# Sending the block sums of v to the query blocks: 128-byte DMA rows against a VectorE copy and 3 KB rows

## The chip, the cores and the metric

The kernel runs on one core of one Trainium2 chip. The metric is the device time of one execution in microseconds (us), as a median over runs. A profiled execution gives the rows below: PE is TensorE, PEld its weight loads, DVE VectorE, ACT ScalarE, POOL GpSimd, SP the engine that issues most of the copies inside the chip's memory and all stores. L306 means line 306 of the kernel before.

## The reference, cut to what matters

Sparse attention over 4 batches of 8 heads, 768 positions and 64 columns, then one expert of a mixture of experts per batch.

```python
block, window = (32, 16)
k_sum = k.reshape(B, H, nb, block, D).max(axis=3)    # nb = 24 blocks
v_sum = v.reshape(B, H, nb, block, D).mean(axis=3)
scores_l = where(|i - j| < window, scale * q @ k.T, -1e9)
scores_s = scale * q @ k_sum.T + log(block)
a = softmax(concat([scores_l, scores_s]))
x = a @ concat([v, v_sum])                           # every query sees all 24 block sums
e = argmax(x.mean(positions) @ w_gate)               # one expert per batch
out = gate * (relu(x @ w1[e]) @ w2[e])
```

## The kernel before, in words

Every head's 768 queries are cut into 12 blocks of 64 (`NJ`). For one block the keys and values that count are 120 rows: its own 64 positions, 16 before and 16 after (the halo), and the 24 block sums. They lie on 120 partitions of the tile `vblk[NR, H, NJ, DP]`, two of them, used by even and odd batches; `DP` is 66, that is 64 columns of v, then the weight by which a row counts in the denominator (1, or 32 for a block sum), and a filler. The weights are written once, in `edges`, lines 154 and 155. The block sums stand on partitions 96 to 119 and are the same for all 12 query blocks of a head, so they lie there 12 times.

A batch is worked through in pairs of heads, four of them (`NP`). The steps of a pair, each a function that is called in an order written out by hand (`attn`, `weave`, `run`; nothing is reordered by a planner):

- `T_k` turns k by TensorE, and VectorE builds the tile `kaug` from it: the copy of line 258, maxima by lines 265 to 273, halos and block maxima by the copies of lines 276, 279 and 282.
- `V_sum` issues the two halo copies on SP (lines 111 and 115), sums v by 12 small products per pair (line 294), casts the sums to bf16 (`vs_sb`, line 303), and sends them on: one DMA on SP for each head (line 306), from 24 partitions, with a broadcast over the 12 query blocks. One such DMA is 288 rows of 128 bytes.
- `T_q` turns q (copies of lines 250 and 252), `S_tile` makes the scores of six query blocks (line 347), ScalarE takes their exponential (`aT`, line 357), and VectorE multiplies by the band mask (line 360; in batch 0 the mask is added by TensorE instead).
- `O_tile` is the product of `aT` and all 120 rows of `vblk` (line 372): 24 matmuls for six query blocks of two heads in two calls. It is what waits for the halo and for the block sums. VectorE then divides (`rv` and `xs`, lines 380 and 383), and `X_tile` turns the result (line 399).

In batch 0 `V_sum` runs pair by pair, one pair ahead of `O_tile` (`pre` in `attn`), so there are four calls with two DMAs each. In batches 1 to 3 it runs once for all four pairs, between the first `T_k` and the first `T_q`, so there are three calls with eight DMAs each. Between the attention steps of batches 1, 2 and 3 the steps of the expert of the batch before are woven in: `H_chunk` (line 477) and `O_chunk` (line 498). The loads of q, k, v (lines 91 and 104) and of the expert's weights (lines 439 and 442) are issued by POOL, which writes their descriptors; those of the next batch and of the weights are issued in one go after `gate`, just when `V_sum` of the next batch runs.

Of the kernel before, what the change touches and what calls it, by code (L numbers as in the profile page):

```python
# [12 lines left out]
BF16 = mybir.dt.bfloat16  # L13
# [9 lines left out]
def kernel(  # L23
# [10 lines left out]
    nc = tc.nc  # L34

    B, H, S, D = q.shape
# [6 lines left out]
    BLK = 32  # L43
    NB = S // BLK
    NJ = S // QB
# [3 lines left out]
    R_SUM = QB + 2 * HALO  # L49
    NR = R_SUM + NB  # L50
# [8 lines left out]
    DP = D + 2  # L59
# [5 lines left out]
    const = ctx.enter_context(tc.tile_pool(name="const", bufs=1))  # L65
# [15 lines left out]
    kaugs = [  # L81
        const.tile([128, NP, NJ, 128], BF16, name=f"kaug{i}") for i in range(2)
    ]


    nat = {}
# [22 lines left out]
    def halo(b, h0, h1):  # L109
        vb = vblks[b % NV]  # L110
        nc.sync.dma_start(
            vb[R_PRE : R_PRE + HALO, h0:h1, 1:NJ, :],
            vb[QB - HALO : QB, h0:h1, 0 : NJ - 1, :],
        )
        nc.sync.dma_start(
            vb[R_POST : R_POST + HALO, h0:h1, 0 : NJ - 1, :],
            vb[0:HALO, h0:h1, 1:NJ, :],
        )
# [78 lines left out]
    )  # L197

    masks = []

    def make_mask():
        lo = const.tile([R_SUM, 1], FP32, name="lo")
        t_a = const.tile([R_SUM, 1], FP32, name="t_a")

        nc.vector.tensor_scalar(
            out=lo, in0=pf[0:R_SUM, :], scalar1=float(R_PRE), scalar2=float(R_PRE + HALO),
            op0=ALU.is_ge, op1=ALU.mult,
        )
        nc.vector.tensor_scalar(
            out=t_a, in0=pf[0:R_SUM, :], scalar1=float(R_POST), scalar2=-float(QB),  # L210
            op0=ALU.is_ge, op1=ALU.mult,
        )
        nc.vector.tensor_tensor(out=lo, in0=lo, in1=t_a, op=ALU.add)
        nc.vector.tensor_scalar(
            out=lo, in0=lo, scalar1=-float(HALO - 1), scalar2=None, op0=ALU.add
        )
        u_f = const.tile([R_SUM, QB], FP32, name="u_f")
        nc.vector.tensor_scalar(
            out=u_f, in0=it_u, scalar1=lo[:, 0:1], scalar2=None, op0=ALU.subtract
        )  # L220
        u_hi = const.tile([R_SUM, QB], FP32, name="u_hi")
        nc.vector.tensor_scalar(
            out=u_hi, in0=u_f, scalar1=float(2 * HALO - 2), scalar2=None, op0=ALU.is_le
        )
        mask = const.tile([NR, QB], BF16, name="mask")
        nc.vector.memset(mask[R_SUM:NR, :], 1.0)
        nc.vector.scalar_tensor_tensor(
            out=mask[0:R_SUM, :], in0=u_f, scalar=0.0, in1=u_hi,
            op0=ALU.is_ge, op1=ALU.mult,
        )  # L230
        masks.append(mask.unsqueeze(1).to_broadcast([NR, 2 * NW, QB]))
# [55 lines left out]
    def V_sum(b, prs):  # L287
        def f():
            vb = vblks[b % NV]
            halo(b, 2 * prs[0], 2 * prs[-1] + 2)  # L290
            vs_ps = one_pool.tile([128, 2, D], FP32, name="vsps", tag="one")
            for j in range(NJ):
                for pr in prs:
                    nc.tensor.matmul(
                        vs_ps[BLK * pr : BLK * (pr + 1), :, :],
                        lhsT=bind[:, j, :],
                        rhs=vb[0:QB, 2 * pr : 2 * pr + 2, j, 0:D],
                        start=(j == 0),
                        stop=(j == NJ - 1),
                    )  # L300
            vs_sb = small.tile([128, 2, D], BF16, name="vs_sb")
            rs = slice(BLK * prs[0], BLK * prs[-1] + BLK)
            nc.vector.tensor_copy(vs_sb[rs], vs_ps[rs])
            for pr in prs:
                for hh in range(2):
                    nc.sync.dma_start(  # L306
                        vb[R_SUM:NR, 2 * pr + hh, :, 0:D],
                        vs_sb[BLK * pr : BLK * pr + NB, hh, :]
                        .unsqueeze(1)
                        .to_broadcast([NB, NJ, D]),  # L310
                    )
        return f

    def T_q(b, pr):
# [313 lines left out]
```

## Time and profile before

| | |
|---|---|
| median of 2 runs | 221.12 us (221.11 to 221.12) |
| the profiled execution | 222.96 us, of which the span is 221.2 us |
| busy: PE, DVE, ACT, POOL | 164.1, 103.8, 85.5, 40.0 us |
| engine shares of the chain that ended last | PE 44%, DMA 20%, DVE 17%, ACT 11% |
| DMAs of line 306 | 32, each 36 KB as 288 rows |

"Idle before" is the time in which an engine stood still just ahead of an instruction, and the name behind the arrow is what ended it. The chain that ended last is followed back from the last instruction; a piece of it named "DMA" begins when that DMA was issued and ends when it let the next instruction go.

### The profile page before, as it was taken

What the parts mean: (1) busy time and instruction counts of PE and PEld (TensorE: products, weight loads), DVE (VectorE), ACT (ScalarE), POOL (GpSimd) and SP (SyncE); (2) the same over time, 40 slices, a digit from 0 to 9 for tenths busy, and PEclk for the clock granted to TensorE, in tenths of its full rate; (3) what the DMA queues carried; (4) which work ended last, traced back from release to release, by engine and by line L of the source; (5) the groups of instructions that cost most, each with busy time, mean ns of one, the idle gap of its engine ahead of it and who ended that gap; (6) DMA issues with size and microseconds to landing.
All of it is one profiled execution on the core that took longest, in us unless ns stands there. A gap on an engine that the chain in (4) does not pass through costs nothing.

```text
span 221.2 us, 5022 instructions
## 1 busy us (share of the span) xinstructions
PE 164.1 (74%) x2094; PEld 97.8 (44%) x2104; DVE 103.8 (47%) x292; ACT 85.5 (39%) x185; POOL 40.0 (18%) x58
## 2 busy tenths in 40 slices
PE   0563983673358889709989789539987899999993
PEld 0453763452334545305444445224444555456541
DVE  5752583267564856704394647521658440210021
ACT  2131560622044475600426474502534765147411
POOL 7981000029400003900000005000000006000000
PEclk9999999999999999975899999955999999999998
DMA  6999997209999950999997403992222009993033
GB/s 59 144 168 200 172 157 109 47 3 127 188 214 153 166 87 9 151 211 206 129 235 202 81 3 48 150 207 38 95 92 98 1 3 94 185 273 115 0 149 135
DMA packets 57574, 27.12 MB, mean 123 GB/s; under 512 B 37072, under 2 KB 54480, under 8 KB 57552
## 3 DMA queue, kind: packets, MB, share of 16 engines
q0 software_dynamic: 42720, 17.83, 83.9%
q1 hardware_dynamic: 14832, 8.98, 17.8%
q8 instruction: 16, 0.26, 0.5%
q14 instruction: 6, 0.05, 0.1%
HBM read 35.67 MB, written 6.29 MB: 190 GB/s over the span
## 4 chain that ended last, share of the span: by engine, by line
PE 44%; DMA 20%; DVE 17%; ACT 11%; issue 3%; POOL 2%; SPq 1%; ACTq 0%; POOLq 0%; DVEq 0%
DMA vblk<-vs_sb 20%; PE o_ps L498 18%; PE hps L477 12%; ACT aT L357 4%; DVE kaug L258 4%; PE ops L372 4%; ACT xT L400 3%; PE qps L241 3%; DVE aT L360 2%; PE xps L399 2%; PE sc L347 2%; DVE t L265 2%; ACT hT L484 1%; DVE kmx L273 1%; SPq L306 1%
## 5 line engine op out<-in xcount | busy, mean ns | idle before, releaser
L477 PE MATMUL hps<-xT,w_sb 128*128 128x384 bf16 x256 | 50.3, 334 | 0.0
L498 PE MATMUL o_ps<-w_sb,hT 128*128 128x512 bf16 x182 | 49.2, 408 | 0.6 <-issue 0.4
L484 ACT ACTIVATE hT<-hps 128x384 bf16<-128x384 f32 x64 | 31.4, 491 | 24.3 <-PE hps L477 24.3
L372 PE MATMUL ops<-vblk,aT 120*64 120x65 bf16 x384 | 14.5, 222 | 33.8 <-DMA vblk<-vs_sb 25.4
L439 POOL DMA_DIRECT2D w_sb<-in_moe_w_dram x14 | 10.5, 760 | 144.0 <-PE hps L477 84.4
L357 ACT ACTIVATE aT<-sc 128x768 bf16<-128x768 f32 x32 | 26.0, 812 | 15.2 <-PE sc L347 14.2
L372 PEld LDWEIGHTS <-aT 120*64 120x64 bf16 x384 | 10.9, 132 | 40.9 <-issue 18.2
L477 PEld LDWEIGHTS <-w_sb 128*128 128x128 bf16 x256 | 22.1, 99 | 13.8 <-issue 0.7
L498 PEld LDWEIGHTS <-hT 128*128 128x128 bf16 x192 | 17.9, 103 | 19.3 <-issue 3.3
L360 DVE TENSOR_TENSOR aT<-aT,mask 120x768 bf16<-120x768 bf16 x24 | 13.3, 556 | 24.4 <-ACT aT L357 24.4
L513 ACT ACTIVATE o_sb<-o_ps,gcol 128x512 f32<-128x512 f32 x12 | 8.2, 687 | 41.9 <-PE o_ps L498 37.8
L400 ACT ACTIVATE xT<-xps 128x384 bf16<-128x384 bf16 x32 | 15.6, 490 | 21.8 <-PE xps L399 21.5
L508 DVE TENSOR_SCALAR o_sb<-o_ps,gcol 128x512 f32<-128x512 f32 x12 | 9.0, 750 | 25.5 <-PE o_ps L498 22.4
L383 DVE TENSOR_TENSOR xs<-ops,rv 128x384 bf16<-128x384 f32 x32 | 17.8, 558 | 1.1
L380 DVE RECIPROCAL rv<-ops 128x6 f32<-128x6 f32 x32 | 6.1, 190 | 25.8 <-PE ops L372 25.6
L258 DVE COPY kaug<-kps 128x768 bf16<-128x768 bf16 x16 | 15.2, 952 | 5.8 <-PE kps L241 5.8
L347 PE MATMUL sc<-qT,kaug 64*128 64x64 bf16 x384 | 13.4, 210 | 5.3 <-DVE qT L252 2.6
L347 PEld LDWEIGHTS <-kaug 64*128 64x128 bf16 x384 | 10.8, 107 | 12.8 <-issue 10.1
L399 PE MATMUL xps<-identb,xs 128*128 128x128 bf16 x96 | 12.9, 256 | 3.2 <-ACT qT L250 1.4
L241 PE MATMUL kps<-identb,k_nat 96*64 96x96 bf16 x256 | 11.1, 245 | 5.0 <-POOL it_p L129 5.0
L252 DVE COPY qT<-qps 128x768 bf16<-128x768 bf16 x12 | 11.4, 952 | 4.7 <-PE qps L241 4.6
L399 PEld LDWEIGHTS <-xs 128*128 128x128 bf16 x96 | 8.4, 111 | 9.6 <-issue 3.1
(71 smaller groups left out, 145.4 us busy)
## 6 DMA issues: line engine op xcount, KB each, us to landing
out_dram<-o_sb SPq DMA_DIRECT2D x24, 256.0 KB
w_sb<-in_moe_w_dram POOLq DMA_DIRECT2D x11, 512.0 KB, 10.9
k_nat<-in_k_dram POOLq DMA_DIRECT2D x3, 768.0 KB, 15.7
vblk<-in_v_dram POOLq DMA_DIRECT2D x6, 384.0 KB, 19.2
q_nat<-in_q_dram POOLq DMA_DIRECT2D x3, 768.0 KB, 23.1
w_sb<-in_moe_w_dram POOLq DMA_DIRECT2D x9, 256.0 KB, 5.6
vblk<-vs_sb SPq DMA_DIRECT2D x32, 36.0 KB
vblk<-vblk SPq DMA_DIRECT2D x6, 181.5 KB
```

The costliest lines, as they stand in the source:

```text
L241: nc.tensor.transpose(ps[hh * D : (hh + 1) * D, r, :], src[:, 2 * pr + hh, r * D : (r + 1) * D], identb[0:PR, 0:PR],)
L258: nc.vector.tensor_copy(ka[:, :, 0:QB].rearrange("q j (p r) -> q j p r", r=RR), ps.rearrange("q r (j p) -> q j p r", j=NJ),)
L347: nc.tensor.matmul(sc[:, hh, w * QB : (w + 1) * QB], lhsT=ka[rs, pr, j, :], rhs=qT[rs, j * QB : (j + 1) * QB], start=not on_pe, stop=not o ...
L357: nc.scalar.activation(aT, sc[:, :, 0:HB], ACT.Exp, scale=SCALE)
L360: nc.vector.tensor_tensor(out=av, in0=av, in1=masks[0], op=ALU.mult)
L372: nc.tensor.matmul(ops[w * QB : (w + 1) * QB, t, hh, :], lhsT=aT[0:NR, hh, c0 : c0 + QB], rhs=vb[0:NR, 2 * pr + hh, u * NW + 2 * t + w, 0 ...
L383: nc.vector.tensor_tensor(out=xs, in0=ops[:, :, :, 0:D], in1=rv.unsqueeze(3).to_broadcast([128, NW // 2, 2, D]), op=ALU.mult,)
L399: nc.tensor.transpose(xps[:, t * 128 : (t + 1) * 128], xs[:, t], identb)
L400: nc.scalar.activation(xT[b][:, pr, u * HB : (u + 1) * HB], xps, ACT.Copy, accum_out=red[b][:, pr, u : u + 1],)
L477: nc.tensor.matmul(hps[:, 0:HB], lhsT=w1_sb[:, dt, ft * 128 : (ft + 1) * 128], rhs=xT[b][:, dt, u * HB : (u + 1) * HB], start=(dt == 0), s ...
L484: nc.scalar.activation(hTs[b][:, ft, u * HB : (u + 1) * HB], hps[:, 0:HB], ACT.Relu)
L498: nc.tensor.matmul(o_ps, lhsT=hTs[b][:, ft, st * 128 : (st + 1) * 128], rhs=w2_sb[:, ft, :], start=(ft == 0), stop=(ft == NFT - 1),)
```

## The change

In batch 0 VectorE writes a pair's sums straight into `vblk`, with one copy that reads `vs_sb` 12 times over. In the other batches one VectorE copy of 128 partitions fills a new tile `vrep`, in which the sums already stand 12 times beside their weight column, and one DMA per pair moves 24 rows of 3,168 bytes (2 heads x 12 blocks x 66 columns x 2 bytes). The weight columns of `vrep` are written once, ahead of the first pair.

```diff
+    vrep = const.tile([128, 2, NJ, DP], BF16, name="vrep")
...
+    nc.vector.memset(vrep[:, :, :, D:DP], float(BLK))
...
             nc.vector.tensor_copy(vs_sb[rs], vs_ps[rs])
+            if len(prs) == 1:
+                pr = prs[0]
+                nc.vector.tensor_copy(
+                    vb[R_SUM:NR, 2 * pr : 2 * pr + 2, :, 0:D],
+                    vs_sb[BLK * pr : BLK * pr + NB]
+                    .unsqueeze(2)
+                    .to_broadcast([NB, 2, NJ, D]),
+                )
+                return
+            nc.vector.tensor_copy(
+                vrep[:, :, :, 0:D], vs_sb.unsqueeze(2).to_broadcast([128, 2, NJ, D])
+            )
             for pr in prs:
-                for hh in range(2):
-                    nc.sync.dma_start(
-                        vb[R_SUM:NR, 2 * pr + hh, :, 0:D],
-                        vs_sb[BLK * pr : BLK * pr + NB, hh, :]
-                        .unsqueeze(1)
-                        .to_broadcast([NB, NJ, D]),
-                    )
+                nc.sync.dma_start(
+                    vb[R_SUM:NR, 2 * pr : 2 * pr + 2, :, :],
+                    vrep[BLK * pr : BLK * pr + NB],
+                )
```

## Rows read from the trace of the kernel before

**Rows 1.** The page: chain by line, and two of its costliest groups.

```profile
DMA vblk<-vs_sb 20%; PE o_ps L498 18%; PE hps L477 12%; ACT aT L357 4%; DVE kaug L258 4%; PE ops L372 4%; ACT xT L400 3%; PE qps L241 3%; DVE aT L360 2%; PE xps L399 2%; PE sc L347 2%; DVE t L265 2%; ACT hT L484 1%; DVE kmx L273 1%; SPq L306 1%
...
L439 POOL DMA_DIRECT2D w_sb<-in_moe_w_dram x14 | 10.5, 760 | 144.0 <-PE hps L477 84.4
...
L258 DVE COPY kaug<-kps 128x768 bf16<-128x768 bf16 x16 | 15.2, 952 | 5.8 <-PE kps L241 5.8
```

**Rows 2.** The waits: us in total, times, longest us.

```profile
PE ops L372 <- DMA vblk<-vs_sb: 25.4, 9, 4.7
```

**Rows 3.** The chain in order of time, batches 2 and 3: start, us, what.

```profile
89.37 10.30 DMA vblk<-vs_sb
...
137.81 9.51 DMA vblk<-vs_sb
```

**Rows 4.** The timeline, two copies of line 276 and 282 in batch 1.

```profile
65.25 0.20 DVE L276 COPY kaug<-kaug 128x176 bf16<-128x176 bf16 x1
...
65.48 0.22 DVE L282 COPY kaug<-kmx 128x288 bf16<-128x288 bf16 x1
```

**Rows 5.** The timeline, batch 1, first pair.

```profile
54.47 2.75 POOL L104 DMA_DIRECT2D vblk<-in_v_dram  x2
...
54.98 0.92 DVE L276 COPY kaug<-kaug 128x176 bf16<-128x176 bf16 x1
...
56.01 0.55 DVE L360 TENSOR_TENSOR aT<-aT,mask 120x768 bf16<-120x768 bf16 x1
...
58.94 0.20 DVE L380 RECIPROCAL rv<-ops 128x6 f32<-128x6 f32 x1 [2.39 <-PE ops L372]
```

**Rows 6.** The timeline, batch 0, first pair: start, us, engine, line, [idle before].

```profile
13.85 2.71 POOL L104 DMA_DIRECT2D vblk<-in_v_dram  x2
...
15.45 0.28 DVE L303 CAST vs_sb<-vsps 32x128 bf16<-32x128 f32 x1
...
19.54 1.23 PE L372 MATMUL ops<-vblk,aT 120*64 120x65 bf16 x24 [4.73 <-DMA vblk<-vs_sb]
...
20.48 0.20 DVE L380 RECIPROCAL rv<-ops 128x6 f32<-128x6 f32 x1 [4.74 <-PE ops L372]
```

**Rows 7.** The DMA queues from 11.8 to 15.0 us: packets, MB, share.

```profile
q1 hardware_dynamic: 132, 0.10, 11.8%
```

**Rows 8.** The timeline, batch 0, third pair.

```profile
33.97 0.30 DVE L303 CAST vs_sb<-vsps 32x128 bf16<-32x128 f32 x1
...
37.60 0.20 DVE L380 RECIPROCAL rv<-ops 128x6 f32<-128x6 f32 x1 [3.33 <-PE ops L372]
```

**Rows 9.** The timeline, first pairs of batch 2 and, last row, of batch 3.

```profile
88.50 12.87 SPq L306 DMA_DIRECT2D vblk<-vs_sb  x8
...
97.70 0.27 PE L372 MATMUL ops<-vblk,aT 120*64 120x65 bf16 x2 [4.70 <-DMA vblk<-vs_sb]
...
99.71 0.82 PE L372 MATMUL ops<-vblk,aT 120*64 120x65 bf16 x22 [1.74 <-DMA vblk<-vs_sb]
...
145.42 0.27 PE L372 MATMUL ops<-vblk,aT 120*64 120x65 bf16 x2 [4.02 <-DMA vblk<-vs_sb]
```

**Rows 10.** Stretches: us, busy (instructions) of PE, PEld, DVE, ACT, POOL, clock, DMA.

```profile
93.00:97.60 4.60, 0.00 (x1) 0.00 (x0) 1.40 (x6) 0.58 (x2) 1.53 (x2) 0.90 1.37 209
97.60:100.00 2.40, 0.56 (x13) 0.47 (x15) 0.00 (x0) 0.00 (x0) 0.00 (x0) 0.50 1.39 213
...
141.00:145.00 4.00, 0.40 (x3) 0.01 (x1) 1.59 (x7) 0.97 (x2) 0.00 (x0) 0.93 1.27 192
```

**Rows 11.** The timeline, the same five PE steps after batch 2's wait, and later.

```profile
100.97 0.61 PE L498 MATMUL o_ps<-w_sb,hT 128*128 128x512 bf16 x1
...
107.10 0.33 PE L399 MATMUL xps<-identb,xs 128*128 128x128 bf16 x3
...
113.36 1.04 PE L498 MATMUL o_ps<-w_sb,hT 128*128 128x512 bf16 x4
...
116.69 0.33 PE L399 MATMUL xps<-identb,xs 128*128 128x128 bf16 x3
```

## The prediction

> **What bounds the kernel now.** I read the page first: a fifth of the chain that ended last is one name, the DMA from `vs_sb` to `vblk` [rows 1]. The waits say who stands still for it: TensorE ahead of line 372, 25.4 us in nine waits [rows 2]. In order of time the chain has five such pieces, in the first and third pair of batch 0 and in the first pair of batches 1, 2 and 3; the longest two are shown [rows 3]. TensorE works in program order, so each of the five holds up all that follows, and the experts' products at the end are TensorE's alone. What a shorter wait gives is therefore kept to the end, unless something else is late at the same place. So I ask at each of the five what would be late next.
>
> **The new copy.** Each call of `V_sum` gets one VectorE copy of 1,536 elements per partition. The trace has none so long between two tiles of SBUF. Copies of 176 and 288 elements take 0.20 and 0.22 us, the longer one with a broadcast like the new one [rows 4]: 112 elements more cost 0.02, so 1,536 cost about 0.22 + 1,248 x 0.18 ns = 0.44 us. The other end is the rate of the copy of 768 elements out of PSUM, 0.95 us [rows 1], hence 1.9 us. I take 0.5, being nearest to the broadcast row. The copy can also be held up. The copy of line 276, 0.20 us alone, took 0.92 and ended 0.05 us after the first of two POOL issues did (54.47 + 2.75/2 = 55.85) [rows 4, 5]. So it costs 0.5 and up to the rest of one POOL issue, 0.76 to 1.4 us [rows 1, 5].
> The Trainium skill, "SBUF — State Buffer", section "SBUF: two separate sides", calls this an exclusive lock between VectorE's faster copies and GpSimd, held for a whole instruction, and that speaks against this change; the trace agrees with 0.92 against 0.20 us. By the rule the sum below stays; without it the two blockings counted below would fall away, about 1.5 us in all.
>
> **Batch 0, first pair.** TensorE is ready at 19.54 - 4.73 = 14.81 [rows 6]. The block sums would lie there by about 11. Next late is the halo: the queue of SP's DMAs moved 0.10 MB from 11.8 to 15.0, and the halo's 64 rows of 1,452 bytes are 0.09 MB, the rest being short rows behind them [rows 7]; I take 15.6 for its landing. Line 372 then starts at 15.65 and its first six blocks are done at about 16.2. But the second pair's copy stands ahead of `rv` on VectorE: the cast ends at 15.73, POOL's issue holds the copy to 13.85 + 2.71 = 16.56, the copy ends near 17.05, and `rv` follows, at 17.05 instead of 20.48 [rows 6]. Gain 3.4 (4.3 if it isn't held). The weight memset at the start, some 0.1 us, is hidden by the wait for the halo. In the step after that the copy delays `rv` by 0.4, which the wait of `X_tile` for ScalarE mostly hides: 0.1 lost.
>
> **Batch 0, third pair.** The halo was free to go long before. `rv` waits instead for the fourth pair's cast, done at 34.27, and the copy: 34.8 instead of 37.60 [rows 8]. Gain 2.9. Batch 0 together: 3.4 - 0.1 + 2.9 = 6.2.
>
> **Batch 1.** The copy stands ahead of the copy of line 252 on VectorE, which feeds the scores. It loses 0.5 and the rest of a POOL issue, about 0.6: scores and mask come 1.1 later. Then line 276 meets the second POOL issue rather than the first (it ends at 57.2), so the second mask product is done at about 58.1 instead of 56.56, and `rv` comes at 58.1 instead of 58.94 [rows 5]. The DMA is no longer last; VectorE is. Gain 0.8. If the copy took 1.9 us this would be a loss of 0.6, with neither blocking a gain of 1.7.
>
> **Batches 2 and 3.** Here the copy costs 0.8 (0.5, and 0.3 of a POOL issue) and the first DMA is issued at 89.3 instead of 88.50. The first DMA before let go at 97.7 and the second at 99.67, both issued by 89.4 [rows 3, 9]: one DMA of 288 short rows took 2.0 us of the slowest engine, and 9.2 - 2.0 = 7.2 us were spent behind the loads. Two dozen long rows, an estimated 0.1 us for the one or two that an engine gets, land at about 89.3 + 7.2 = 96.5 (say 96.4, as the issue is shorter). Both calls of line 372 follow in 0.8: done at 97.2 instead of 100.53. Gain 3.3. In batch 3 the first wait ended at 145.4 and the second at 147.3, 1.9 apart [rows 3, 9]; the first issue is taken 0.87 ahead of the second, as in batch 2, at 136.94. So 8.5 - 1.9 = 6.6 after an issue at 137.7 gives 144.3, done at 145.1 instead of 148.2. Gain 3.1. The second mask product, some 0.9 us later than before, is still done ahead of both landings.
> On SP the three other DMAs queue behind the first, and nothing waits for SP there: it is done within 3 us where it took 12.87 [rows 9].
>
> **The clock.** After the wait of batch 2 the granted clock is 0.50, that is 1.2 GHz. The mean of 0.90 over 93.0 to 97.6 puts the fall at 97.6 - 0.9 = 96.7, after 3.7 us without a matmul; in batch 3 0.93 puts it at 144.4, after 3.0 [rows 9, 10]. Five PE steps (three chunks of line 498, one turning of q, one `X_tile`) then took 107.10 - 100.97 = 6.13 us; the same five at full clock took 116.69 - 113.36 = 3.33 [rows 11]. That is 2.8 us, in batch 3 alike. With the change TensorE would stand still for some 2.8 us in batch 2 (93.6 to 96.4) and 2.3 in batch 3 (142.0 to 144.3). Both are shorter than what came before a fall, so I let the clock hold: 2 x 2.8 = 5.6.
>
> **The sum.** 6.2 + 0.8 + 3.3 + 3.1 + 5.6 = 19.0 us. The profiled execution took 222.96 (span 221.2, 1.8 around it) and would take 204.0. The median of the runs shown is 1.84 lower, and I take the same 19.0 from it: 202.1, rounded to 202.
>
> **Rivals.**
> 1. The clock still falls. For it: 2.8 us of standing still is close to 3.0. Against: no gap of that size was followed by a fall in the full-clock part of the trace. In one batch: 205; in both: 221.1 - 13.4 = 207.7.
> 2. The long rows land little sooner. What was waited for may be the turn of SP's queue behind the loads, and not 288 rows. If a DMA saves half of the 2.0 us, it lands at 97.4 and 145.2, line 372 is done at 98.25 and 146.05 (gains 2.3 and 2.1), the waits are 3.8 and 3.2 and the clock falls: 6.2 + 0.8 + 4.4 = 11.4, 209.7. If it saves nothing (98.4 and 146.2), 9.5: 211.6. For it: 7.2 of 9.2 us passed before the rows themselves counted. Against: the second DMA's own 2.0.
> The Trainium skill, "DMA: Bandwidth & Descriptors", section "Queues, rings and completion order", has each DMA engine change between queues after a packet of some 9 to 17 descriptors; by that rule short rows go several to a turn, and the result would be the 209.7 above.
> 3. The copy is slow, up to 1.9 us. Five copies stand on the path (second and fourth pair of batch 0, batches 1 to 3), so 1.4 more each cost 7, and the clock perhaps 5.6: 209 to 215. For it: 66-column steps and a broadcast in one copy, which no row has. Against: line 282 [rows 4].
> 4. The copy is so slow that the kernel loses. With the clock falling as before, 13.4 us are gained and 5 x (t - 0.5) lost, so it decides at t = 3.2 us, 2.1 ns per element; at 4 us the time is 225. The slowest copy in the trace has 1.24 ns per element [rows 1], so little speaks for it.
>
> **How the numbers follow.** Forecast 0.45, rival 1 0.27, rival 2 0.16, rival 3 0.07, rival 4 0.03; 0.02 remains for more, a halo that lands earlier and copies that are never held (197). The range goes from 197 to 211, leaving out the end of rival 2, half of rival 3 and rival 4. The forecast's own range is 199 to 205. A measurement here tells about 2% from no change, so faster means below 216.7: all cases but rival 4 and the far end of rival 3, that is 0.94, with 0.03 each for the other two.
>
> **What would show it.** Right: no DMA of the block sums in the chain of waits of batches 0 and 1; line 372 first at about 15.7 us; a copy of 0.4 to 0.6 us where POOL is quiet; the first DMA of batches 2 and 3 let go 6 to 7.5 us after its issue; a granted clock of 1.00 after both. Wrong: a wait of over 3 us left ahead of line 372 in batch 2 or 3, a copy over 1 us, or `rv` of the first pair still near 20 us.

## The result and the profile after

The changed kernel takes 209.52 us (median of 2 runs, 209.06 and 209.98) against 221.12: a ratio of 0.948 (95% interval 0.939 to 0.957), so 11.6 us or 5.2% less. The profiled execution took 209.98 with a span of 208.3, where that of before took 222.96 with 221.2. The forecast was 202.0, the range 197 to 211. The ratios leave out an execution that took over 1.5% longer than the fastest of its kernel, while the medians and spreads count all.

The lines have moved by 3 to 12: line 372 of before is L384 now, `rv` L392, the first mask product L372, the cast of `vs_sb` L306, the new direct copy L309, the copy into `vrep` L316 and the DMA L320.

The page: the granted clock by slices, the chain by engine, and the group that waits.

```profile
PEclk9999999999999999957999999859999999999999
...
PE 46%; DVE 29%; ACT 10%; DMA 8%; issue 3%; POOL 2%; DVEq 0%; ACTq 0%; POOLq 0%
...
L384 PE MATMUL ops<-vblk,aT 120*64 120x65 bf16 x384 | 13.7, 223 | 18.5 <-DMA vblk<-vrep 7.9
```

DMA has gone from 20% of the chain to 8%, and VectorE from 17% to 29%. But 8% of 208.3 is still 16 us, and the clock falls twice (the digits 5 and 7, and 8 and 5). The waits and the chain say where:

```profile
PE ops L384 <- DMA vblk<-vrep: 7.9, 2, 4.3
```

```profile
81.28 8.44 DMA vblk<-vrep
...
127.37 7.71 DMA vblk<-vrep
```

Of nine waits for the block sums with 25.4 us in all [rows 2] two are left (in batch 0 the first pair waits 0.18 us for the halo, and in batch 1 VectorE is last, 2.02 and 0.69 us), and of the five DMA pieces of the chain two. They are the longest ones of before, in the first pairs of batches 2 and 3, and each is shorter by less than 2 us (10.30 and 9.51 [rows 3] against 8.44 and 7.71).

To see where the 12.9 us of span came from, take a mark that both kernels have: the first matmuls that turn k in batches 1, 2 and 3 (timeline of TensorE: start, us; three rows of before, then three of now):

```profile
46.13 0.85 PE L241 MATMUL kps<-identb,k_nat 96*64 96x96 bf16 x16
...
85.30 0.53 PE L241 MATMUL kps<-identb,k_nat 96*64 96x96 bf16 x16
...
133.69 0.53 PE L241 MATMUL kps<-identb,k_nat 96*64 96x96 bf16 x16
...
39.98 0.85 PE L244 MATMUL kps<-identb,k_nat 96*64 96x96 bf16 x16
...
77.39 0.53 PE L244 MATMUL kps<-identb,k_nat 96*64 96x96 bf16 x16
...
123.43 0.53 PE L244 MATMUL kps<-identb,k_nat 96*64 96x96 bf16 x16
```

| stretch | before | after | gain | forecast |
|---|---|---|---|---|
| to the mark of batch 1 (batch 0) | 46.13 | 39.98 | 6.15 | 6.2 |
| to the mark of batch 2 (batch 1) | 39.17 | 37.41 | 1.76 | 0.8 |
| to the mark of batch 3 (batch 2) | 48.39 | 46.04 | 2.35 | 3.3 + 2.8 |
| to the end of the span (batch 3, last expert) | 87.51 | 84.87 | 2.64 | 3.1 + 2.8 |

Batch 0 is on the forecast, batch 1 better, and batches 2 and 3 lack 7.0 us. There the first DMA is issued at 81.28, after a copy of 0.66 us, and TensorE waits 4.33 us for it (timeline of batch 2, with POOL's weight loads, and the last row of batch 3):

```profile
78.62 2.25 POOL L451 DMA_DIRECT2D w_sb<-in_moe_w_dram  x3 [26.45 <-DVE grec L465]
...
80.59 0.66 DVE L316 COPY vrep<-vs_sb 128x1536 bf16<-128x1536 bf16 x1
...
81.28 3.54 SPq L320 DMA_DIRECT2D vblk<-vrep  x4
...
89.86 0.87 PE L384 MATMUL ops<-vblk,aT 120*64 120x65 bf16 x24 [4.33 <-DMA vblk<-vrep]
...
135.21 0.87 PE L384 MATMUL ops<-vblk,aT 120*64 120x65 bf16 x24 [3.60 <-DMA vblk<-vrep]
```

All 24 matmuls now go together (x24), where before two went and 22 waited for the second DMA [rows 9]: the second DMA's wait is gone, and the first one's is nearly whole. The first row gives the hint. POOL's first weight load began there, and at these times in batch 3 and in the kernel before (timelines of POOL: batch 3 now, then batches 2 and 3 before):

```profile
124.71 2.25 POOL L451 DMA_DIRECT2D w_sb<-in_moe_w_dram  x3 [38.09 <-PE hps L489]
...
86.53 2.25 POOL L439 DMA_DIRECT2D w_sb<-in_moe_w_dram  x3 [28.54 <-DVE grec L453]
...
134.98 2.25 POOL L439 DMA_DIRECT2D w_sb<-in_moe_w_dram  x3 [40.45 <-PE hps L477]
```

From POOL's first weight load to the first matmul of line 384 it is 89.86 - 78.62 = 11.24 us, and before it was 97.70 - 86.53 = 11.17. In batch 3 it is 135.21 - 124.71 = 10.50, and before it was 145.42 - 134.98 = 10.44. The landing stands at the same distance from the loads, though the rows and the time of issue differ. (Between traces of the same code this distance varies more: it was 10.36 in batch 2 of one run below.)

The DMA queues say what happened in between (packets, MB, share; first from 80.5 to 85.5 us, where q1, the queue of SP's copies, has no row at all, then q1 from 87.5 to 89.9):

```profile
q0 software_dynamic: 1192, 0.68, 116.0%
...
q1 hardware_dynamic: 102, 0.21, 40.5%
```

For 4.2 us after the issue not one packet of SP's copies moved; all 1,192 of the first window belonged to loads that POOL had issued (q0).

And the clock (stretches: us; busy time and instructions of PE, PEld, DVE, ACT, POOL; granted clock; DMA share; GB/s):

```profile
85.00:93.00 8.00, 3.67 (x36) 1.80 (x33) 3.50 (x12) 1.10 (x3) 1.62 (x2) 0.77 1.21 205
93.00:100.00 7.00, 7.00 (x69) 3.60 (x69) 2.46 (x4) 2.55 (x6) 0.00 (x0) 0.78 2.20 179
132.00:141.00 9.00, 5.79 (x54) 3.20 (x55) 3.31 (x11) 0.32 (x2) 0.00 (x0) 0.62 1.06 181
```

A mean of 0.62 over 9 us means 0.38 x 9 / 0.5 = 6.8 us at the level of 0.50 (1.2 GHz); 0.77 and 0.78 make 3.7 + 3.1 = 6.8 us too. Four matmuls of a chunk took 1.89 us in it (at 93.77), and 1.04 at full clock (at 143.11).

### The profile page after: what moved, and what is told of

Read it like the earlier page. It is cut to its first block, busy times and chain, and to the rows that moved or that the text cites. A ratio compares the mean times of both kernels' runs of the same rounds, so it can differ in the third digit from the quotient of the medians.

```text
span 208.3 us, 5017 instructions
## 1 busy us (share of the span) xinstructions
PE 163.6 (79%) x2104; PEld 96.7 (46%) x2104; DVE 108.2 (52%) x300; ACT 85.8 (41%) x185; POOL 40.3 (19%) x58
## 3 DMA queue, kind: packets, MB, share of 16 engines
q0 software_dynamic: 42720, 17.83, 86.7%
## 4 chain that ended last, share of the span: by engine, by line
PE 46%; DVE 29%; ACT 10%; DMA 8%; issue 3%; POOL 2%; DVEq 0%; ACTq 0%; POOLq 0%
PE o_ps L510 19%; PE hps L489 14%; DMA vblk<-vrep 8%; DVE kaug L261 6%; ACT aT L369 5%; ACT xT L412 3%; DVE aT L372 3%; DVE xs L395 3%; PE ops L384 3%; DVE t L268 2%; PE sc L359 2%; PE qps L244 2%; DVE kmx L276 2%; PE xps L411 2%; DVE t L272 2%
## 5 line engine op out<-in xcount | busy, mean ns | idle before, releaser
L384 PE MATMUL ops<-vblk,aT 120*64 120x65 bf16 x384 | 13.7, 223 | 18.5 <-DMA vblk<-vrep 7.9
L372 DVE TENSOR_TENSOR aT<-aT,mask 120x768 bf16<-120x768 bf16 x24 | 13.3, 553 | 24.7 <-ACT aT L369 24.7
L384 PEld LDWEIGHTS <-aT 120*64 120x64 bf16 x384 | 10.5, 132 | 25.6 <-DVE aT L372 10.6
L244 PE MATMUL kps<-identb,k_nat 96*64 96x96 bf16 x256 | 11.1, 245 | 5.2 <-DMA k_nat<-in_k_dram 5.2
L411 PEld LDWEIGHTS <-xs 128*128 128x128 bf16 x96 | 8.0, 109 | 11.8 <-DVE xs L395 5.9
L244 PEld LDWEIGHTS <-k_nat 96*64 96x64 bf16 x256 | 8.5, 136 | 9.3 <-DMA k_nat<-in_k_dram 5.2
## 6 DMA issues: line engine op xcount, KB each, us to landing
w_sb<-in_moe_w_dram POOLq DMA_DIRECT2D x11, 512.0 KB, 11.5
q_nat<-in_q_dram POOLq DMA_DIRECT2D x3, 768.0 KB, 22.5
```

The costliest lines, as they stand in the source:

```text
L244: nc.tensor.transpose(ps[hh * D : (hh + 1) * D, r, :], src[:, 2 * pr + hh, r * D : (r + 1) * D], identb[0:PR, 0:PR],)
L372: nc.vector.tensor_tensor(out=av, in0=av, in1=masks[0], op=ALU.mult)
L384: nc.tensor.matmul(ops[w * QB : (w + 1) * QB, t, hh, :], lhsT=aT[0:NR, hh, c0 : c0 + QB], rhs=vb[0:NR, 2 * pr + hh, u * NW + 2 * t + w, 0 ...
L411: nc.tensor.transpose(xps[:, t * 128 : (t + 1) * 128], xs[:, t], identb)
```

## The experiments

Theory 1: in batches 2 and 3 the DMA of the block sums waits for its turn behind the loads that POOL issued before it, and what one DMA then costs is a turn, however long its rows are. Theory 2: the time is in the rows, and the new ones are less quick than I took them for. Each run compares with runs of the kernel before on the same chip: 221.3 us for the first four kernels, 221.26 for the next four, 219.74 for the last two.

**The change in halves.** Batch 0 alone (VectorE's direct copy there, the 128-byte rows everywhere else):

```diff
-            nc.vector.tensor_copy(
-                vrep[:, :, :, 0:D], vs_sb.unsqueeze(2).to_broadcast([128, 2, NJ, D])
-            )
             for pr in prs:
-                nc.sync.dma_start(
-                    vb[R_SUM:NR, 2 * pr : 2 * pr + 2, :, :],
-                    vrep[BLK * pr : BLK * pr + NB],
-                )
+                for hh in range(2):
+                    nc.sync.dma_start(
+                        vb[R_SUM:NR, 2 * pr + hh, :, 0:D],
...
```

> Only batch 0 has the VectorE copy; batches 1 to 3 send 128-byte rows as before. If the parts add up, this alone gains the 6.1 us by which batch 1 begins earlier in the changed kernel's profile: about 215 us, with the waits of batches 1 to 3 as before (2.8+2.3, 4.7+1.7 and 4.0+1.7 us) and the clock falling after the last two. Rival: the gain of batch 0 is partly lost again in later waits for loads, 217 us or more.

Measured: 214.69 us, ratio 0.975 (0.967 to 0.983), 6.6 less. The three long pieces of batches 1 to 3 are back in its chain of waits (6.81 us in batch 1, and):

```profile
82.38 9.43 DMA vblk<-vs_sb
...
129.30 9.05 DMA vblk<-vs_sb
```

Batches 1 to 3 alone (`vrep` and long rows there, the two DMAs per pair in batch 0):

```diff
             if len(prs) == 1:
-                pr = prs[0]
-                nc.vector.tensor_copy(
-                    vb[R_SUM:NR, 2 * pr : 2 * pr + 2, :, 0:D],
...
+                for pr in prs:
+                    for hh in range(2):
+                        nc.sync.dma_start(
+                            vb[R_SUM:NR, 2 * pr + hh, :, 0:D],
...
```

> Only batches 1 to 3 have the copy into vrep and the 3 KB rows; batch 0 sends 128-byte rows as before. If the parts add up: 221.1 - 6.8 = about 214.3 us, with the two waits of batch 0 (4.7 and 3.4 us) as before. If the long rows themselves were worth what I had forecast for batches 1 to 3, it would be 208.

Measured: 216.79 us, ratio 0.986 (0.977 to 0.996), 4.5 less and not the 7 expected. Its profiled execution took 216.03, 6.9 under that of before, but it was the quickest of the four runs. With the other half's 6.6 this makes 11.1, and the whole change again (below) 11.2: the halves add up. The half that moves the data in long rows gave less than the one that gives up the DMA, but by the two intervals (0.967 to 0.983, 0.977 to 0.996) this difference is not clear of noise.

**Weights behind the copy.** The kernel after, but in batches 2 and 3 POOL issues the weight loads and the next batch's k only after it has read a corner of `vrep`, which VectorE finishes as SP's first DMA is issued:

```diff
+    def later(b):
+        if b < 2:
+            return
+        peek = small.tile([1, 2], BF16, name="peek")
+        nc.gpsimd.tensor_copy(peek, vrep[0:1, 1, NJ - 1, D - 2 : D])
+        gate_loads(b - 1)
+        if b + 1 < B:
+            load_k(b + 1)
...
                     vrep[BLK * pr : BLK * pr + NB],
                 )
+            later(b)
```

`gate_loads` holds the weight loads, cut out of `gate`.

> In batches 2 and 3 POOL issues the expert's weight loads and the next k load only when VectorE's copy into vrep is done, some 2.7 us later; the same DMAs otherwise. Theory 1 (the block sums' DMA waits for its turn behind weight loads that were issued before it; its rows cost little): the first one lands 2 to 4 us after its issue instead of 8, TensorE waits for the mask product instead, the clock stays at 1.00, and the time is 198 to 202 us. Theory 2 (the time lies in the 24 rows, their 3 KB or the writes into vblk): it lands 7 us or more after its issue and the time stays at 209 to 211.

Measured: 198.84 us (198.48 to 199.17), ratio 0.902 (0.894 to 0.910). That is 22.5 us under before, twice what the change itself gave. Timeline of batch 2:

```profile
81.24 4.59 SPq L320 DMA_DIRECT2D vblk<-vrep  x4
...
81.89 2.25 POOL L434 DMA_DIRECT2D w_sb<-in_moe_w_dram  x3 [0.44 <-issue]
...
85.42 0.38 PE L385 MATMUL ops<-vblk,aT 120*64 120x65 bf16 x12
...
87.03 0.38 PE L385 MATMUL ops<-vblk,aT 120*64 120x65 bf16 x12 [1.22 <-DVE aT L373]
```

The same DMA issued at the same time (81.24 against 81.28): in batches 2 and 3 nothing waits for it any more, and the second call waits for VectorE's mask. (In batch 1, where the order is the old one, the first pair waits 1.88 us for its DMA.) The DMA queues from 80.5 to 83.6 us show that it had gone by then (its 24 rows of 3,168 bytes are 0.08 MB):

```profile
q1 hardware_dynamic: 36, 0.08, 10.9%
```

So 2.4 us after its issue, against 8.6 with the loads ahead of it. The mean clock is 0.995. This is theory 1's result.

**TensorE kept busy through the wait.** 18 matmuls into a tile that nothing reads, ahead of the first `O_tile` of batches 2 and 3; nothing else is changed:

```diff
+            if b > 1 and pr == 0 and u == 0:
+                warm = one_pool.tile([128, 512], FP32, name="warm", tag="one")
+                for _ in range(18):
+                    nc.tensor.matmul(
+                        warm[:, 0:HB],
+                        lhsT=identb,
+                        rhs=ident6.rearrange("p w c -> p (w c)"),
...
```

> Ahead of the first O_tile of batches 2 and 3, 18 matmuls of 384 columns into a PSUM tile that nothing reads are added, about 2.9 us of TensorE inside waits of 4.3 and 3.6 us. If the clock falls because TensorE stands still there, the granted clock stays at 1.00, the waits end when they did, and the time falls by the price of the clock, 2 x 2.2 to 2.8 us: about 204 to 205. If the fall has another cause, the clock falls all the same and the time stays at 209 to 210.

Measured: 204.15 us, ratio 0.925 (0.917 to 0.934). The clock holds (the page; then TensorE's timeline in batch 2: the first matmul of line 384, L394 here, and the second `X_tile`, and as the last row that `X_tile` in the kernel after):

```profile
PEclk9999999999999999999999999999999999999998
```

```profile
88.71 0.57 PE L394 MATMUL ops<-vblk,aT 120*64 120x65 bf16 x24 [0.52 <-DMA vblk<-vrep]
...
92.85 0.33 PE L421 MATMUL xps<-identb,xs 128*128 128x128 bf16 x3
...
96.83 0.33 PE L411 MATMUL xps<-identb,xs 128*128 128x128 bf16 x3
```

Against the kernel after (209.52 and 210.03 in its two comparisons) this is 5.4 to 5.9 us less. Not all of it is the clock: in batch 2 the DMA came 0.9 us sooner (10.36 us from the first load, against 11.24; in batch 3 10.54 against 10.50). From the first matmul of line 384 to the second `X_tile` it is 92.85 - 88.71 = 4.14 us, in batch 3 the same, and in the kernel after 96.83 - 89.86 = 6.97 and, in batch 3, 141.70 - 135.21 = 6.49. So the two falls cost 5.2 us, where the forecast had 5.6.

**No DMA at all.** VectorE writes the sums straight into `vblk` in every batch: the first pair in `V_sum`, the others one pair ahead, behind `xs`; `vrep` is gone.

```diff
+    def put(b, pr):
+        nc.vector.tensor_copy(
+            vblks[b % NV][R_SUM:NR, 2 * pr : 2 * pr + 2, :, 0:D],
+            vss[b][BLK * pr : BLK * pr + NB].unsqueeze(2).to_broadcast([NB, 2, NJ, D]),
+        )
...
+            if b > 0 and u == 1 and pr + 1 < NP:
+                put(b, pr + 1)
```

> No DMA carries block sums any more: in batches 1 to 3 VectorE copies the first pair's sums straight into vblk inside V_sum and each further pair's after the pair before it is divided (four copies of 24 partitions instead of one of 128 and four DMAs); POOL's order is that of the changed kernel. Theory 1 (the wait was the DMA's turn): no wait for a DMA is left ahead of O_tile in batches 1 to 3, the clock stays at 1.00, and 5 to 6 us each are gained in batches 2 and 3, less up to 3 x 0.55 us in batch 1, where VectorE is late: 198 to 201 us. If instead something else ends those waits at the same time (the halo, or a load), the time stays at 207 to 210.

Measured: 200.1 us, ratio 0.907 (0.901 to 0.913). What TensorE waits for ahead of this line is VectorE's mask now:

```profile
PE ops L384 <- DVE aT L372: 12.0, 10, 2.5
```

So taking the DMA away is worth about as much as letting it go first. But the clock, expected at 1.00, fell once in this trace, in batch 2, after a wait of 1.27 us ahead of this line (stretch from 80 to 110 us, as above; a mean of 0.94 is 3.6 us at 0.50):

```profile
80.00:110.00 30.00, 25.97 (x334) 13.35 (x331) 21.33 (x54) 11.98 (x24) 6.91 (x8) 0.94 1.39 195
```

**Short rows in the good order.** The kernel with the weights behind the copy, but in batches 1 to 3 the block sums go as before, two DMAs per pair of 288 rows of 128 bytes; POOL reads a corner of `vs_sb` instead:

```diff
-            nc.vector.tensor_copy(
-                vrep[:, :, :, 0:D], vs_sb.unsqueeze(2).to_broadcast([128, 2, NJ, D])
-            )
...
+                for hh in range(2):
+                    nc.sync.dma_start(
+                        vb[R_SUM:NR, 2 * pr + hh, :, 0:D],
...
+            later(b, vs_sb)
```

> As the run with the weights behind the copy, but with the old 128-byte rows, two DMAs a pair, and no vrep in batches 1 to 3; POOL's loads of batches 2 and 3 wait for the cast of the block sums. Theory 1 (the turn counts, the rows hardly): the first DMA lands within 3 to 4 us and the second, issued beside the first load, within one turn; the waits end near the mask product, the clock stays at 1.00, and the time is 198 to 202, no worse than with the long rows. Theory 2 (288 short rows cost what they cost): waits of 2 us and more stay in both batches and the time is 204 or more.

Measured: 202.27 us (201.36 to 205.44), ratio 0.914 (0.905 to 0.922); the median without the 205.44 is 201.90. This is at the upper end of what theory 1 gave and below theory 2's 204, and the trace says why. Timeline of batch 2, the stretch from 80 to 110 us, and the DMA queue from 82.0 to 84.8 us:

```profile
82.46 8.93 SPq L316 DMA_DIRECT2D vblk<-vs_sb  x8
...
86.90 0.22 PE L383 MATMUL ops<-vblk,aT 120*64 120x65 bf16 x2
...
89.21 0.54 PE L383 MATMUL ops<-vblk,aT 120*64 120x65 bf16 x22 [2.09 <-DMA vblk<-vs_sb]
```

```profile
80.00:110.00 30.00, 26.59 (x370) 13.69 (x368) 19.13 (x47) 12.52 (x26) 8.18 (x10) 0.94 1.38 168
```

```profile
q1 hardware_dynamic: 300, 0.04, 8.0%
```

Within 2.3 us of its issue the first DMA's 288 rows (0.04 MB) had gone, as soon as the 24 long ones (2.4 us). What is late is the second DMA: by the chain it is issued at 83.33, 0.87 us behind the first, and POOL's first weight load began at 83.11. Its wait is 2.09 us in batch 2, as theory 2 had it, and 0.45 in batch 3. After the wait in batch 2 the clock fell for some 3.6 us. So in this order the long rows are worth one DMA instead of two for a pair; what they are worth beside the loads is told below.

**Small weight loads.** The kernel after with one line changed: w1 of batches 1 to 3 in eight loads of 128 columns, instead of three of 256, 256 and 512.

```diff
-        cuts = [0, 1, 2, 4, 6, 8] if b == 0 else [0, 2, 4, 8]
+        cuts = [0, 1, 2, 4, 6, 8] if b == 0 else list(range(9))
```

> The changed kernel with the first expert weight of batches 1 to 3 loaded in eight DMAs of 128 columns instead of three of 256, 256 and 512. If a turn of the loads' queue is as long as one DMA's share of an engine, the turns ahead of the block sums shrink, and their first DMA lands 4 to 6 us after its issue instead of 8; the waits fall below 3 us and the time to 204 to 207. If a turn does not depend on the size of the loads' DMAs, it lands after 7.5 to 8.5 us as before, and the time is 209 to 211 (POOL issues five more loads).

Measured: 199.57 us, ratio 0.905 (0.898 to 0.912), more than I expected. The order is that of the kernel after, and the DMA went between 83 and 85 us (q0 from 78.5 to 82.9, where q1 has no row, then q1 from 83.0 to 85.0), 1.8 to 3.8 us after its issue:

```profile
81.19 3.15 SPq L320 DMA_DIRECT2D vblk<-vrep  x4
...
85.36 0.38 PE L384 MATMUL ops<-vblk,aT 120*64 120x65 bf16 x12
```

```profile
q0 software_dynamic: 1444, 0.36, 84.0%
...
q1 hardware_dynamic: 51, 0.11, 18.1%
```

Smaller loads let the DMA through sooner. Why is not told apart: the loads and their rows are smaller, and as POOL takes 0.76 to 0.78 us to issue a load of either size, less is issued ahead of the DMA (three loads of 128 KB by 81.19, against 256 + 256 + 512 KB by 81.28 in the kernel after).

**The changed kernel again**, beside the three above.

> The changed kernel once more, beside the others on one chip: 209 to 210 us, with the first DMA of batches 2 and 3 let go 7.5 to 8.5 us after its issue and the clock at 0.50 after it.

Measured: 210.03 us, ratio 0.951 (0.944 to 0.957). In this trace the first pair of batch 1 waits for its DMA too (3.36 us, to 6.08 us after the issue): VectorE and the DMA are nearly level there.

**Both remedies**, and **the one line in the kernel before.**

> Both edits that removed the wait together: weight loads behind the copy, and eight loads of 128 columns. With either alone the mask product is what TensorE waits for, so nothing is left to gain at the first pairs: 198 to 200 us. The later pairs' DMAs, which in the reordered run still take turns beside the loads (one wait of 1.9 us), come sooner: at best 197. If the loads of the next batch, now later by both edits, become late: 201 or more.

Measured: 200.42 us (198.52 to 202.02), ratio 0.916 (0.908 to 0.923): a little over the 198 to 200 expected. Either remedy takes the wait away, and the second finds nothing left.

> The kernel before with one line changed: the first expert weight of batches 1 to 3 in eight loads of 128 columns. Theory 1: the two DMAs of 128-byte rows get their turns behind shorter loads, the second lands 5 to 6 us after the first's issue instead of 10, the waits of batches 2 and 3 shrink to 1 us or less, the clock holds, and 12 to 16 us are gained, though batch 0 still waits for its DMAs: 205 to 210 us. If the short rows themselves are what takes the time, 2 to 4 us remain of each wait and 216 us or more are measured.

Measured: 209.87 us (207.4 to 213.59), ratio 0.957 (0.949 to 0.965). In batch 2 the DMA piece of the chain is 5.43 us instead of 10.30 [rows 3], and the waits are 1.25 and 0.37 instead of 4.70 and 1.74 [rows 9], the first of them:

```profile
94.02 0.22 PE L372 MATMUL ops<-vblk,aT 120*64 120x65 bf16 x2 [1.25 <-DMA vblk<-vs_sb]
```

One line of cuts, with all the short rows left as they were, gives 9.9 us, nearly as much as the whole change (11.2 beside it). What it cannot give is batch 0: both long pieces (8.94 and 9.11 us) are still in its chain.

## Why the prediction was right or wrong

The time lies in the range, but not by the forecast's own case (199 to 205): it is that of rival 2, which had a chance of 0.16. The forecast's sign of being wrong, a wait of over 3 us left in batch 2 or 3, came in both.

**Batch 0 was right.** It was to gain 6.2 and gained 6.15; alone, 6.6. The first pair (timeline):

```profile
14.98 0.87 PE L384 MATMUL ops<-vblk,aT 120*64 120x65 bf16 x24 [0.18 <-DMA vblk<-vblk]
...
16.08 0.90 DVE L309 COPY vblk<-vs_sb 24x1536 bf16<-24x1536 bf16 x1
...
17.01 0.20 DVE L392 RECIPROCAL rv<-ops 128x6 f32<-128x6 f32 x1
...
31.70 0.20 DVE L392 RECIPROCAL rv<-ops 128x6 f32<-128x6 f32 x1
```

TensorE starts at 14.98 (forecast 15.65; the halo was earlier than I took it for), and `rv` still comes at 17.01 (forecast 17.05), because the next pair's copy on VectorE is last, held up by POOL as foreseen. It was another POOL issue than the one I named: the q load, which POOL issued from 15.84 to 16.62. In the third pair `rv` comes at 31.70 instead of 37.60 [rows 8]: 5.9 us, of which the first pair's `rv` had 3.5 already, so 2.4 more where I had 2.9 - 0.1 (34.8 against 37.60 is 2.8, not 2.9).

**The copy was right**: 0.5 forecast, 0.55 alone, 0.66 and 0.68 in batches 2 and 3 and 0.90 beside a POOL issue. That rules out rivals 3 and 4.

**Batch 1 was sized too low** (0.8 forecast, 1.76 found). The step that failed is "It loses 0.5 and the rest of a POOL issue, about 0.6". The copy took 0.56, and it seems that POOL was held instead: one of the issues of line 451 beside VectorE's copies lasted 1,082 ns, where 762 is the median.

```profile
43.12 3.31 POOL L451 DMA_DIRECT2D w_sb<-in_moe_w_dram  x4 [0.17 <-issue]
...
44.09 0.56 DVE L316 COPY vrep<-vs_sb 128x1536 bf16<-128x1536 bf16 x1
...
50.66 0.18 DVE L392 RECIPROCAL rv<-ops 128x6 f32<-128x6 f32 x1
```

`rv` of the first pair came at 50.66, 10.68 us after the batch's mark, where before it was 12.81 (58.94 [rows 5] less 46.13). VectorE being last was right in this trace, but narrowly: in the traces of all six other runs with long rows the first call waits for the DMA there, 1.88 to 3.36 us, and in the changed kernel's second one `rv` came 11.5 us after the mark.

**Batches 2 and 3 were wrong**, at the second half of the step "one DMA of 288 short rows took 2.0 us of the slowest engine, and 9.2 - 2.0 = 7.2 us were spent behind the loads". The forecast let these 7.2 us run from the DMA's issue and stay as long when the copy put the issue off. The DMA was let go 8.6 and 7.8 us after its issue (the forecast had 7.2 and 6.6), and its distance from the weight loads stayed the same to 0.07 us. That is the result of rival 2. Both calls were done at 90.73, 9.45 us after the issue, against 12.03 before (100.53 less 88.50): 2.6 less, of which the copy takes 0.7 back.

Rival 2's reason, that long rows save little, is not what the DMA queues show. POOL's queue in the two kernels, from the first load until SP's first packet moves (86.5 to 92.0 us before, 78.6 to 86.5 now), and both queues before, from 97.7 to 99.7 us:

```profile
q0 software_dynamic: 1040, 0.54, 85.0%
...
q0 software_dynamic: 1381, 0.86, 90.3%
...
q0 software_dynamic: 391, 0.39, 114.5%
q1 hardware_dynamic: 290, 0.04, 23.0%
```

In the 2.0 us between two landings before, 290 packets of SP's, one DMA's rows, moved beside 391 of POOL's: beside loads the short rows did take these 2.0 us, though 288 of them are gone 2.3 us after their issue when nothing is ahead. With long rows nearly three DMAs (0.21 MB) went in the 2.4 us from 87.5 to 89.9. The 9.2 us before were 3.6 from the issue to SP's first packet, at 92.1, and 5.6 from there to the first matmul; the 8.6 now are 5.4, to 86.7, and 3.2 (in batch 3, 4.8 and 3.7 before, 5.3 and 2.6 now). So the rows did get through sooner, and what they saved was lost ahead of them. Before, POOL had issued two loads when SP issued its DMA (0.52 MB; the third was under way), now three (1.05 MB): the 0.7 us of the copy had let a load of 512 KB go ahead. The term that failed is thus the time behind the loads. That SP's DMA begins when about as much has moved as was issued ahead of it fits the traces (0.54 and, in batch 3, 0.68 MB before, 0.86 and 0.89 now, 0.36 with small loads), but no run varies the time of issue alone: why the start came later, and whether it is chance that it cancels the gain to 0.07 us, stays open.

**The clock** followed from the waits, as rival 2 had it. They were 4.33 and 3.60 us, rival 2 had 3.8 and 3.2, the forecast 2.8 and 2.3; the granted clock fell to 0.50 in both, and the 2 x 2.8 = 5.6 us didn't come. The price was nearly right (5.2). The step "Both are shorter than what came before a fall, so I let the clock hold" was unsafe in itself: no run has waits of 2.8 and 2.3, but the clock fell after a wait of 2.09 us (short rows in the good order) and after one of 1.27 (no DMA at all), when the matmuls had already gone on, and it held after one of 1.22 (weights behind the copy). These are the profiled executions; the clock's mean over others of the same kernels goes up to 1.00.

**The sum.** Rival 2 with half of the 2.0 us saved gave 209.7, with nothing saved 211.6; 209.5 came. That the half case fits so well is luck. Counted from the first load both calls were done 1.9 and 1.8 us sooner (it had 2.3 and 2.1); the falls cost less than before (the five steps [rows 11] took 5.66 us from 91.17 and 5.17 from 136.53, against 6.13 and, in batch 3 before, 6.19); batch 1 gave 1.0 more; and the profiled executions differ by 13.0, the medians by 11.6. Of the 19.0 us forecast 13.0 came in the profiled execution: 1.0 more in batch 1, 2.7 less by the landings of batches 2 and 3 (3.7 of 6.4), and the rest, 4.3 less, by the clock.

The Trainium skill, "DMA: Bandwidth & Descriptors", section "Queues, rings and completion order", has a DMA engine change between queues by packets of some 9 to 17 descriptors. The long standstill does not agree with that, if a packet of the trace is one descriptor: in the 4.2 us after the issue POOL's queue moved 986 packets, over 60 for each of 16 engines, and SP's none. How many descriptors make a turn no run here shows.

## What to carry to other kernels

When a small DMA is waited for while bulk loads are under way, count the DMAs that go one behind the other and see what was issued ahead of them; making their rows longer helps only if the rows' own time is what one waits for, and a step that puts the issue off can let more bulk go ahead and take the gain back. Two cures are cheap: issue the small copy first and the bulk behind it (22.5 us here, with the change), or cut the bulk loads smaller (one line; nearly as much as the whole change by itself, and with it as good as the first cure). And a wait that ends in a fall of the clock costs twice, so a forecast has to carry the fall as part of the wait and not as a case of its own: here it came after waits of 1.27 us and more.

## What the runs showed of the hardware that I had not expected

- A queue with work issued can stand still altogether while another has loads: 0 packets in the 4.2 us after the issue, although 24 rows need 2.4 us when nothing is ahead of them.
- Loads in halves and quarters cost nothing that shows: 15 more issues on POOL (29 instead of 14 of line 451, 789 and 782 ns each in the mean) and the kernel is 10 us quicker.
- The granted clock can fall after TensorE has gone on: with a wait of 2.09 us that ended at 89.21, stretches of 0.5 us show it at 1.00 until 90.5 and at 0.50 from 91.0 to 93.5.
- Beside VectorE's copies a POOL issue took 1,082 ns instead of 762, as a copy beside a POOL issue took 0.90 us instead of 0.55: each seems to hold the other.
- One VectorE copy moves 24 partitions to partitions 96 to 119 and repeats them 12 times in 0.55 us, 0.36 ns per element; the same to 128 partitions takes 0.56.
